# Mixture of experts after a chunked recurrence: one tile per step with its own weights, against two tiles per expert in a fixed order

## The chip, the cores and the metric

The kernel runs on one core of a Trainium2 chip. The metric is the device time of one execution in microseconds (us), a median over runs. The core has TensorE (PE, with its weight loads shown apart as PEld), VectorE (DVE), ScalarE (ACT), GpSimd (POOL) and SyncE (SP), which only issues transfers. All numbers are float32.

## The reference, cut to what matters

Part one is a recurrence over 768 steps for 4 batches of 8 heads with 40 by 40 states. Part two is a mixture of 16 experts in 4 groups; each of the 3072 tokens goes to one expert.

```python
for t in range(S):                                    # 768 steps
    y[:, :, t] = einsum('bhd,bhde->bhe', rt, state)
    Sa = einsum('bhde,bhe->bhd', state, at)
    state = state * wt[:, :, None, :] - einsum('bhd,bhe->bhde', Sa, bt) + einsum('bhd,bhe->bhde', vt, kt)
x = y.transpose(0, 2, 1, 3).reshape(3072, 320)
g_idx = argmax(x @ w_group)                           # 4 groups, softmax weight g_w
e_idx = argmax(xg @ w_expert[g])                      # 4 experts in the group, softmax weight e_w
h = maximum(xg[mask_e] @ w1[g, e], 0)                 # 320 -> 1024
out[tok_idx] = (g_w * e_w)[:, None] * (h @ w2[g, e])  # 1024 -> 320
```

With the reference's inputs the 16 experts get between 152 and 229 tokens each (204, 162, 213, 198, 203, 229, 197, 178, 211, 189, 202, 213, 152, 180, 174, 167), worked out from the reference.

## The kernel before, in words

**Part one** (lines 142 to 363) takes the recurrence in 24 chunks of 128 steps (6 chunks for each of 4 batches, the batches in turn). Each chunk loads six transposed inputs (`in_w`, `in_a`, `in_k`, `in_b`, `in_v`, `in_r`, three sets of buffers) and `vn` (two buffers) on SP's queue, forms triangular products, inverts by seven squarings (lines 267 to 299), and leaves 128 rows of the token matrix in `x_all`, which stays in SBUF. `gate_logits` transposes these rows and multiplies them with the gate weights. A check (lines 351 to 363) leaves two loop counts for a step-by-step version of the recurrence (lines 369 to 432); with these inputs both are zero.

**Routing** (lines 434 to 530) turns the gate logits of all tokens into a one-hot of 16 experts, counts with two matmuls against `up` and `ones`, gives every expert whole tiles of 128 rows in a DRAM buffer `xs`, and writes each token's row there, with its gate weight and number, by 24 indirect transfers on POOL's queue (line 528). `xs` was filled with blank rows at the start (line 189).

**The experts** (lines 532 to 572) are a loop over all NT = 39 tiles that could be needed. Each tile reads its expert's number from `ex_i`, loads that expert's 2,560 KB of weights (three buffers), loads its 128 rows (`xt`), transposes them, multiplies with `w1` (24 products of 128 columns, two matmul records each, 8 of the 24 on only 64 rows, since 320 = 128 + 128 + 64), applies relu, multiplies with `w2` (8 products of 320 columns, two records each), scales by the gate weight and writes the rows to `out` with an indirect transfer on POOL's queue.

The framework's scheduler sets the order of instructions on each engine and queue: an engine's queue runs in order, but that order is not the order of the program text. Tiles with `bufs=n` rotate over n buffers, and a load waits until the last reader of its buffer is done.

Of the kernel before, what the change touches and what calls it, by code (L numbers as in the profile page):

```python
# [25 lines left out]
def kernel(  # L26
# [28 lines left out]
    FG = 4  # L55
# [4 lines left out]
    XW = DM + 2  # L60
    NT = (NTOK + NE * (P - 1)) // P
# [21 lines left out]
    # up[s, t] = 1 for s < t; low[t, s] = 1 for s < t  # L83
# [13 lines left out]
    nc.gpsimd.iota(x_all[:, :, DM + 1:], pattern=[[P, NN], [1, 1]], base=0, channel_multiplier=1,  # L97
                   allow_small_or_imprecise_dtypes=True)
# [6 lines left out]
    # Rows sorted by expert, each expert's share filled up to whole tiles. Rows that no token  # L105
    # takes keep a zero vector and a number beyond the last token.
    xs = dpool.tile([NT * P, XW], F32, name="xs")
    blank = cpool.tile([P, XW], F32, name="blank")
    nc.vector.memset(blank, 0.0)
    nc.vector.memset(blank[:, DM + 1:], float(2 * NTOK))  # L110
# [16 lines left out]
    def gate_logits(pool, n):  # L127
        t = transpose_x(pool, x_all[:, n, :])
# [7 lines left out]
    # With P_t the product of w over the chunk's steps before t and Q_t that product through t,  # L136
    # A = a P, K = k / Q, B = b / Q and S the state at the chunk's start:
    #   (I + T) U = A S' + G V,         T[t, s] = B_s . A_t,  G[t, s] = K_s . A_t   (s < t)
    #   Y = P (R S + M K - N B),        M[t, s] = r_t . v_s,  N[t, s] = r_t . u_s   (s < t)
    #   next S = (S + V' K - U' B) Q_last  # L140
    # and (I + T)^-1 = (I - T)(I + T^2)(I + T^4)... exactly, T being strictly triangular.
    with ExitStack() as part:
# [18 lines left out]
        # The states of a pair of heads stand as the two diagonal blocks of a square that is zero  # L161
        # elsewhere: ST with the second axis of a state on the partitions, SN with the first.
# [14 lines left out]
        for u in range(NN):  # L177
# [4 lines left out]
            if u < NB:  # L182
                # the partitions that no head's rows take
# [14 lines left out]
            # the running products of w (within its bounds), and a, k, b scaled by them  # L198
# [57 lines left out]
            # the right-hand side, then a factor of the inverse at a time  # L256
# [52 lines left out]
            # the next state  # L309
# [13 lines left out]
            # what the chunk returns  # L323
            NTm = [product(UT, Rt, g, up4, "NT", 4) for g in GR]
            ps = small([P, H, D])
            for i in range(NP):
# [3 lines left out]
                for j in range(2):  # L330
# [19 lines left out]
            gate_logits(sb, n)  # L350

        # how often the bounds are broken
# [16 lines left out]
    with ExitStack() as part:  # L369
        sq = part.enter_context(tc.tile_pool(name="seq", bufs=1))  # L370
        x_seq = dpool.tile([NTOK, DM], F32, name="x_seq")
# [3 lines left out]
        # partition (q, b, h) holds rows q DQ .. (q + 1) DQ of the state of (b, h)  # L375
# [13 lines left out]
        with tc.For_i(0, n_seq, 1) as i:  # L389
# [34 lines left out]
            for b_ in range(B):  # L424
                r0 = nc.s_assert_within(s0 + b_ * S, 0, NTOK - TB)
                nc.sync.dma_start(out=x_seq[ds(r0, TB), :].rearrange("t (h d) -> h t d", h=H),
                                  in_=ys[b_ * H:(b_ + 1) * H])

        with tc.For_i(0, n_back, 1):
            nc.sync.dma_start(out=x_all[:, :, :DM], in_=x_seq.rearrange("(n p) d -> p n d", p=P))  # L430
            for n in range(NN):
                gate_logits(sq, n)

# [1 line left out]
    with ExitStack() as part:  # L435
# [6 lines left out]
        nc.gpsimd.iota(thr, pattern=[[P, NN]], base=0, channel_multiplier=0,  # L442
# [3 lines left out]
                       allow_small_or_imprecise_dtypes=True)  # L446
# [31 lines left out]
        nc.vector.tensor_tensor(x_all[:, :, DM], wtg, wte, op=ALU.mult)  # L478
        oh = gp.tile([P, NN, NE], F32, name="oh")
        for g in range(G):  # L480
# [3 lines left out]
        # each token's rank within its expert, then its row in xs  # L484
# [14 lines left out]
        cmp = gp.tile([P, NE, NN], F32, name="cmp")  # L499
        nc.vector.tensor_tensor(cmp, inc[:, :, NN - 1:].broadcast_to([P, NE, NN]),  # L500
                                thr[:, None, :].broadcast_to([P, NE, NN]), op=ALU.is_gt)
# [4 lines left out]
        base = gp.tile([P, NE, 1], F32, name="base")  # L506
        nc.vector.tensor_tensor(base[:, :, 0], tend, tiles, op=ALU.subtract)
        nc.vector.tensor_scalar(base, base, float(P), None, op0=ALU.mult)
        nc.vector.tensor_tensor(tot, tot, base.broadcast_to([P, NE, NN]), op=ALU.add)
        slot = gp.tile([P, NN, NE], F32, name="slot")  # L510
        nc.vector.tensor_tensor(slot, pr, tot.rearrange("p e n -> p n e"), op=ALU.add)
        nc.vector.tensor_tensor(slot, slot, oh, op=ALU.mult)
        pos = gp.tile([P, NN], F32, name="pos")
        nc.vector.tensor_reduce(out=pos, in_=slot, axis=AX.X, op=ALU.add)
        pos_i = cpool.tile([P, NN], I32, name="pos_i")
        nc.vector.tensor_copy(out=pos_i, in_=pos)

        # each tile's expert
        past = gp.tile([P, NT, NE], F32, name="past")
        nc.vector.tensor_tensor(past, tidx[:, :, None].broadcast_to([P, NT, NE]),  # L520
# [79 lines left out]
```

## Time and profile before

| what | value |
|---|---|
| median of 3 runs | 2348.99 us (2346.05 to 2349.27) |
| span of the profiled execution | 2344.1 us |
| TensorE busy | 2137.4 us (91%) |
| VectorE, ScalarE, GpSimd busy | 636.2, 416.2, 188.8 us |
| bytes moved | 152.68 MB, 65 GB/s over the span |
| mean granted TensorE clock | 0.806 of full |

The span runs from the first to the last instruction; the times of the runs are those of whole executions, 2.0 to 5.2 us longer than this span. The profiled execution's own whole time is not listed apart. The granted clock is 1.00 for 2.4 GHz and 0.50 for 1.2 GHz; a value between is a stretch with both.

### The profile page before, as it was taken

To read this page: it belongs to the slowest core of one execution; us is meant where nothing else is said; L and a number is where in the kernel's file an instruction comes from. 1 tells how busy PE (TensorE), PEld (TensorE's weight loads), DVE (VectorE), ACT (ScalarE), POOL (GpSimd) and SP (SyncE) were. 2 spreads that over 40 slices of the span, in tenths; PEclk is the share of its full clock that TensorE was granted. 3 is DMA by queue.
4 is the path that set the end of the run, shared out by engine and by line. 5 is a ranking of instruction groups with operands and counts; after the bars stand their busy time and mean duration, and the time that the engine had idled before them with its cause. 6 is when DMAs were issued, how large, how long until landed. Compare 5 with 4: busy or idle time off the path is not lost. (4 is left out here: it accounts for less than half of the span.)

```text
span 2344.1 us, 32451 instructions
## 1 busy us (share of the span) xinstructions
PE 2137.4 (91%) x13731; PEld 1943.0 (83%) x13731; DVE 636.2 (27%) x1156; ACT 416.2 (18%) x766; POOL 188.8 (8%) x190
## 2 busy tenths in 40 slices
PE   4999999999999999999999999999505999999998
PEld 3999999999999999999999999999404677777676
DVE  6423333332333333233333232222300111111111
ACT  2222222121222212122212122222000000000000
POOL 3000000000000000000000000000021000000000
PEclk9878876687877868787767787777656999999999
DMA  6000000000000000000000000000042666666661
GB/s 186 21 12 18 21 17 19 20 18 12 18 18 18 21 21 18 12 18 18 18 21 18 12 13 18 4 1 1 29 155 88 212 212 215 200 202 217 205 212 51
DMA packets 143699, 152.68 MB, mean 65 GB/s; under 512 B 33529, under 2 KB 129534, under 8 KB 143552
## 3 DMA queue, kind: packets, MB, share of 16 engines
q1 hardware_dynamic: 133824, 136.21, 18.9%
q10 hardware_dynamic: 6704, 6.46, 1.0%
q0 software_dynamic: 3024, 7.90, 0.9%
q8 instruction: 111, 1.82, 0.3%
q14 instruction: 36, 0.29, 0.0%
HBM read 136.22 MB, written 16.78 MB: 65 GB/s over the span
## 5 line engine op out<-in xcount | busy, mean ns | idle before, releaser
L558 PE MATMUL big<-xT,w1s 128*128 128x128 f32 x1872 | 338.9, 312 | 25.3 <-DVE xT L122 24.6
L558 PEld LDWEIGHTS big<-xT,w1s 128*128 128x128 f32 x1872 | 259.3, 191 | 108.0 <-DVE xT L122 34.7
L293 PE MATMUL small<-U,ET 128*128 128x40 f32 x2688 | 345.9, 290 | 0.6 <-ACT ET L276 0.4
L293 PEld LDWEIGHTS small<-U,ET 128*128 128x128 f32 x2688 | 340.8, 205 | 2.3 <-ACT ET L276 0.5
L273 PE MATMUL big<-ET,E 128*128 128x128 f32 x2304 | 336.6, 292 | 0.0
L273 PEld LDWEIGHTS big<-ET,E 128*128 128x128 f32 x2304 | 300.7, 204 | 0.0
L282 PE MATMUL big<-E,ET 128*128 128x128 f32 x1920 | 266.0, 284 | 0.0
L276 ACT COPY ET<-big 128x512 f32<-128x512 f32 x288 | 168.8, 586 | 481.2 <-PE big L273 481.2
L282 PEld LDWEIGHTS big<-E,ET 128*128 128x128 f32 x1920 | 247.3, 201 | 0.0
L299 DVE TENSOR_TENSOR U<-U,small 128x320 f32<-128x320 f32 x168 | 80.7, 480 | 457.4 <-PE small L293 457.4
L566 PE MATMUL small<-w2s,hT 128*128 128x320 f32 x624 | 180.5, 443 | 0.0
L566 PEld LDWEIGHTS small<-w2s,hT 128*128 128x128 f32 x624 | 116.6, 192 | 48.9 <-issue 1.6
L244 POOL TENSOR_TENSOR E<-E,fit 128x512 f32<-128x512 f32 x48 | 48.9, 1039 | 1199.5 <-DVE fit L242 1188.8
L561 DVE TENSOR_SCALAR hT<-big 128x512 f32<-128x512 f32 x39 | 27.0, 692 | 342.6 <-PE big L558 342.6
L124 ACT COPY xT<-big 64x128 f32<-64x128 f32 x63 | 16.3, 259 | 565.2 <-DVE xT L122 565.2
L120 PE MATMUL big<-ident,xt 128*128 128x128 f32 (+1 forms) x117 | 19.6, 277 | 96.4 <-DMA xt<-xs 96.4
L225 PE MATMUL big<-in_a,in_k 40*128 40x128 f32 x384 | 89.0, 447 | 18.1 <-DMA in_r<-in_rT_dram 18.1
L120 PEld LDWEIGHTS big<-ident,xt 128*128 128x128 f32 (+1 forms) x117 | 14.2, 133 | 105.4 <-DMA xt<-xs 97.5
L334 PE MATMUL small<-nB,NT 128*128 128x40 f32 x384 | 98.6, 351 | 0.0
L225 PEld LDWEIGHTS big<-in_a,in_k 40*128 40x128 f32 x384 | 75.1, 322 | 27.8 <-POOL in_k L212 18.1
L332 PE MATMUL small<-Kn,MT 128*128 128x40 f32 x384 | 94.4, 339 | 0.0
L263 PE MATMUL small<-vn,GT 128*128 128x40 f32 x384 | 94.1, 402 | 0.0
(166 smaller groups left out, 2302.5 us busy)
## 6 DMA issues: line engine op xcount, KB each, us to landing
w2s<-in_w_dram SPq DMA_DIRECT2D x39, 1280.0 KB
w1s<-in_w_dram SPq DMA_DIRECT2D x39, 1024.0 KB
w1s<-in_w_dram SPq DMA_DIRECT2D x39, 256.0 KB
xs<-blank ACTq DMA_DIRECT2D x1, 6279.0 KB
xt<-xs SPq DMA_DIRECT2D x39, 161.0 KB
vn<-in_v_dram SPq DMA_DIRECT2D x24, 160.0 KB
in_w<-in_wT_dram SPq DMA_DIRECT2D x48, 80.0 KB
in_a<-in_aT_dram SPq DMA_DIRECT2D x48, 80.0 KB
```

The lines of the kernel that those rows point to most:

```text
L225: nc.tensor.matmul(ps[:, q, :], lhsT=lhs[blk(g), q, :], rhs=rhs[blk(g), q, :], start=True, stop=True)
L244: nc.gpsimd.tensor_tensor(E[g], E[g], fit.broadcast_to([P, NP, P]), op=ALU.mult)
L263: nc.tensor.matmul(ps[:, 2 * i + j, :], lhsT=GT[j][:, i, :], rhs=vn[:, 2 * i + j, :], start=(c == 0), stop=(c == 0 or j == 1))
L273: nc.tensor.matmul(ps[:, q, :], lhsT=E[g][:, q, :], rhs=ET[g][:, q, :], start=True, stop=True)
L276: nc.scalar.copy(out=t, in_=ps)
L282: nc.tensor.matmul(ps[:, q, :], lhsT=ET[g][:, q, :], rhs=E[g][:, q, :], start=True, stop=True)
L293: nc.tensor.matmul(ps[:, h, :], lhsT=ET[h % 2][:, h // 2, :], rhs=U[:, h, :], start=True, stop=True)
L299: nc.vector.tensor_tensor(nx, U, ps, op=ALU.add if lv else ALU.subtract)
L332: nc.tensor.matmul(o, lhsT=MT[j][:, i, :], rhs=Kn[:, i, blk(j)], start=(c == 0), stop=False)
L334: nc.tensor.matmul(o, lhsT=NTm[j][:, i, :], rhs=nB[:, i, blk(j)], start=False, stop=(c == 0 or j == 1))
L558: nc.tensor.matmul(ps[:, f, :], lhsT=w1s[:kn, ko, (f0 + f) * P:(f0 + f + 1) * P], rhs=xT[:kn, ko, :], start=(ko == 0), stop=(ko == NK - 1))
L566: nc.tensor.matmul(ps, lhsT=hT[:, f, :], rhs=w2s[:, f, :], start=(f == 0), stop=(f == FQ - 1))
```

## The change

Token rows go from each chunk to a DRAM buffer `x_nat` in token order. Routing no longer moves rows. It gives every expert two tiles (TE = 2), and further tiles (up to NOV = 22) to experts with more than 256 tokens. One-hot matmuls over the 24 blocks of tokens give, for each row of each of the 54 possible tiles, the token's number and gate weight. The experts run in the order 0 to 15, both tiles together, with weights loaded once; rows are gathered from `x_nat` by index. The third part of `w1` and of the transposed rows is filled up with zeros to 128 rows. The weights of experts 0 and 1 are loaded during part one. A loop whose count is read on the chip takes further tiles.

```diff
-    x_all = cpool.tile([P, NN, XW], F32, name="x_all")
+    x_nat = dpool.tile([NTOK, DM], F32, name="x_nat")
...
+    WE = 2
+    KR = KO[-1][1]
+    wbuf = []
+
+    def weight_buffers(pool):
+        i = len(wbuf)
+        w1s = pool.tile([P, NK, F], F32, name=f"w1s{i}", bufs=1)
+        w2s = pool.tile([P, FQ, DM], F32, name=f"w2s{i}", bufs=1)
+        nc.gpsimd.memset(w1s[KR:, NK - 1, :], 0.0)
+        wbuf.append((w1s, w2s))
+
+    for i in range(WE):
+        weight_buffers(cpool)
+
+    def load_weights(e, buf):
+        w1s, w2s = buf
+        nc.sync.dma_start(out=w1s[:, :NK - 1, :],
+                          in_=w1_flat[ds(e * DM, (NK - 1) * P), :].rearrange("(o p) f -> p o f", p=P))
+        nc.sync.dma_start(out=w1s[:KR, NK - 1, :], in_=w1_flat[ds(e * DM + (NK - 1) * P, KR), :])
+        nc.sync.dma_start(out=w2s, in_=w2_flat[ds(e * F, F), :].rearrange("(o p) d -> p o d", p=P))
...
-            if u == NB:
-                nc.scalar.dma_start(out=xs.rearrange("(j p) d -> p j d", p=P),
-                                    in_=blank[:, None, :].broadcast_to([P, NT, XW]))
+            if NB < u <= NB + WE:
+                load_weights(u - NB - 1, wbuf[u - NB - 1])
...
+            xn = sb.tile([P, DM], F32, name="xn")
...
-            gate_logits(sb, n)
-
-        # how often the bounds are broken
+            nc.sync.dma_start(out=x_nat[n * P:(n + 1) * P, :], in_=xn)
+            gate_logits(sb, xn, n)
...
+        slot = gp.tile([P, NN, NE], F32, name="slot")
+        nc.vector.tensor_tensor(slot, pr, tot.rearrange("p e n -> p n e"), op=ALU.add)
+        nc.vector.tensor_tensor(slot, slot, oh, op=ALU.mult)
+        rank = gp.tile([P, NN], F32, name="rank")
+        nc.vector.tensor_reduce(out=rank, in_=slot, axis=AX.X, op=ALU.add)
...
+        ov_t = gp.tile([P, NE], F32, name="ov_t")
+        nc.vector.tensor_tensor(ov_t, tend, tiles, op=ALU.subtract)
+        nc.vector.tensor_scalar(ov_t, ov_t, float(NM - TE), None, op0=ALU.add)
+        nc.vector.tensor_tensor(ov_t, ov_t, own_t, op=ALU.subtract)
+
+
+        ge = gp.tile([P, NN, NN], F32, name="ge")
+        nc.vector.tensor_tensor(ge, rank[:, :, None].broadcast_to([P, NN, NN]),
+                                thr[:, None, :].broadcast_to([P, NN, NN]), op=ALU.is_ge)
+        nth = gp.tile([P, NN], F32, name="nth")
+        nc.vector.tensor_reduce(out=nth, in_=ge, axis=AX.X, op=ALU.add)
...
+        nc.vector.tensor_tensor(slot, oh, ov_t[:, None, :].broadcast_to([P, NN, NE]), op=ALU.mult)
+        nc.vector.tensor_reduce(out=tl, in_=slot, axis=AX.X, op=ALU.add)
+        nc.vector.tensor_tensor(tl, tl, ge[:, :, TE - 1], op=ALU.mult)
+        nc.vector.tensor_tensor(slot, oh, own_t[:, None, :].broadcast_to([P, NN, NE]), op=ALU.mult)
+        nc.vector.tensor_reduce(out=rank, in_=slot, axis=AX.X, op=ALU.add)
+        nc.vector.tensor_tensor(tl, tl, rank, op=ALU.add)
+        nc.vector.tensor_tensor(tl, tl, nth, op=ALU.add)
+
+
+        oh_row = gp.tile([P, NN, P], F32, name="oh_row")
+        nc.vector.tensor_tensor(oh_row, row[:, :, None].broadcast_to([P, NN, P]),
+                                lane[:, None, :].broadcast_to([P, NN, P]), op=ALU.is_equal)
+        what = gp.tile([P, NN, 2, NT], F32, name="what")
+        nc.vector.tensor_tensor(what[:, :, 1, :], tl[:, :, None].broadcast_to([P, NN, NT]),
+                                tidx[:, None, :].broadcast_to([P, NN, NT]), op=ALU.is_equal)
+        nc.gpsimd.tensor_tensor(what[:, :, 0, :], what[:, :, 1, :],
+                                tok1[:, :, None].broadcast_to([P, NN, NT]), op=ALU.mult)
+        nc.vector.tensor_tensor(what[:, :, 1, :], what[:, :, 1, :],
+                                gw[:, :, None].broadcast_to([P, NN, NT]), op=ALU.mult)
+        ps = small([P, 2, NT])
+        for n in range(NN):
+            nc.tensor.matmul(ps.rearrange("p a j -> p (a j)"), lhsT=oh_row[:, n, :],
+                             rhs=what[:, n, :, :].rearrange("p a j -> p (a j)"),
+                             start=(n == 0), stop=(n == NN - 1))
...
-        for n in range(NN):
-            nc.gpsimd.indirect_dma_start(
-                out=xs[:, :], out_offset=bass.IndirectOffsetOnAxis(ap=pos_i[:, n:n + 1], axis=0),
-                in_=x_all[:, n, :], in_offset=None)
...
+        fp = part.enter_context(tc.tile_pool(name="ffn", bufs=2))
+        weight_buffers(fp)
+        WB = len(wbuf)
+        XB = []
+        for i in range(2):
+            t = fp.tile([P, NK, TE * P], F32, name=f"xT{i}", bufs=1)
+            nc.gpsimd.memset(t[KR:, NK - 1, :], 0.0)
+            XB.append(t)
+
+        def ffn(buf, xT, cols, weight, dst):
+
+            w1s, w2s = buf
+            n_t = len(cols)
+            w = n_t * P
+            per = 512 // w
+            for t_, col in enumerate(cols):
+                xt = fp.tile([P, DM], F32, name="xt", bufs=4)
+                nc.gpsimd.indirect_dma_start(
+                    out=xt, out_offset=None, in_=x_nat[:, :],
+                    in_offset=bass.IndirectOffsetOnAxis(ap=col, axis=0))
+                pt = big([P, NK, P])
+                for ko, (k0, kn) in enumerate(KO):
+                    nc.tensor.transpose(pt[:kn, ko, :], xt[:, k0:k0 + kn], ident)
+                sl = slice(t_ * P, (t_ + 1) * P)
+                nc.vector.tensor_copy(out=xT[:, :NK - 1, sl], in_=pt[:, :NK - 1, :])
+                nc.scalar.copy(out=xT[:KR, NK - 1, sl], in_=pt[:KR, NK - 1, :])
+            hT = fp.tile([P, FQ, TE * P], F32, name="hT")
+            for f0 in range(0, FQ, per):
+                ps = big([P, per, w])
+                for f in range(per):
+                    for ko in range(NK):
+                        nc.tensor.matmul(ps[:, f, :], lhsT=w1s[:, ko, (f0 + f) * P:(f0 + f + 1) * P],
+                                         rhs=xT[:, ko, :w], start=(ko == 0), stop=(ko == NK - 1))
...
+            for t_ in range(n_t):
+                ps = small([P, DM])
+                for f in range(FQ):
+                    nc.tensor.matmul(ps, lhsT=hT[:, f, t_ * P:(t_ + 1) * P], rhs=w2s[:, f, :],
+                                     start=(f == 0), stop=(f == FQ - 1))
+                yt = fp.tile([P, DM], F32, name="yt", bufs=3)
+                nc.vector.tensor_scalar(yt, ps, weight[t_], None, op0=ALU.mult)
+                nc.gpsimd.indirect_dma_start(
+                    out=out[:, :], out_offset=bass.IndirectOffsetOnAxis(ap=dst[t_], axis=0),
+                    in_=yt, in_offset=None, bounds_check=NTOK - 1, oob_is_err=False)
...
+        for e in range(NE):
+            if e >= WE:
+                load_weights(e, wbuf[e % WB])
+            js = range(e * TE, (e + 1) * TE)
+            ffn(wbuf[e % WB], XB[e % 2], [column(src_i, j) for j in js],
+                [column(w_row, j) for j in js], [column(dst_i, j) for j in js])
+
+
+        n_over = nc.values_load(n_ov[0:1, 0:1], min_val=0, max_val=NOV)
+        with tc.For_i(0, n_over, 1) as j:
```

## Rows read from the trace of the kernel before

**Rows 1.** The page's first line: span and instructions.
```profile
span 2344.1 us, 32451 instructions
```
**Rows 2.** Stretches: us, busy time (instructions) by engine, clock, DMA share, GB/s.
```profile
0.00:18.10 18.10, 0.00 (x0) 0.00 (x0) 15.25 (x28) 11.62 (x18) 11.21 (x30) 1.00 0.66 173
...
1670.00:1693.00 23.00, 3.03 (x5) 1.18 (x4) 14.88 (x51) 0.74 (x3) 0.38 (x3) 0.50 0.01 3
1693.00:1782.50 89.50, 0.91 (x4) 0.49 (x4) 0.86 (x4) 0.23 (x1) 23.19 (x24) 0.50 0.42 138
1782.50:1805.00 22.50, 21.94 (x67) 15.90 (x67) 1.54 (x3) 0.63 (x2) 0.02 (x1) 0.57 0.18 59
1805.00:2336.20 531.20, 507.16 (x2543) 373.69 (x2543) 61.13 (x149) 32.55 (x76) 37.36 (x38) 1.00 0.60 195
2336.20:2344.10 7.90, 0.00 (x0) 0.00 (x0) 0.55 (x1) 0.00 (x0) 0.98 (x1) 0.80 0.00 0
```
**Rows 3.** Timeline of one expert tile: start us, us, engine, line, instruction [idle before].
```profile
1805.08 8.52 PE L558 MATMUL big<-xT,w1s 128*128 128x128 f32 x48 [0.65 <-DVE xT L122]
...
1813.54 4.58 PE L566 MATMUL small<-w2s,hT 128*128 128x320 f32 x16
...
1817.95 0.49 PE L120 MATMUL big<-ident,xt 128*128 128x128 f32 x3
...
1819.09 8.52 PE L558 MATMUL big<-xT,w1s 128*128 128x128 f32 x48 [0.65 <-DVE xT L122]
```
**Rows 4.** Timeline of PE's weight loads at the first tile's start.
```profile
1782.46 0.93 PEld L558 LDWEIGHTS big<-xT,w1s 128*128 128x128 f32 x4 [1.14 <-issue]
1783.61 0.50 PEld L558 LDWEIGHTS big<-xT,w1s 64*128 64x128 f32 x2 [0.22 <-issue]
1784.34 0.93 PEld L558 LDWEIGHTS big<-xT,w1s 128*128 128x128 f32 x4 [0.23 <-issue]
```
**Rows 5.** Timeline of PE's weight loads in part one, at full clock.
```profile
1648.74 1.87 PEld L273 LDWEIGHTS big<-ET,E 128*128 128x128 f32 x16
```
**Rows 6.** Timeline of DVE in the routing.
```profile
1686.61 0.55 DVE L500 TENSOR_TENSOR cmp<-inc,thr 128x384 f32<-128x384 f32 x1
...
1688.10 0.80 DVE L520 TENSOR_TENSOR past<-tidx,tend 128x624 f32<-128x624 f32 x1
...
1690.24 1.09 DVE L511 TENSOR_TENSOR slot<-small,tot 128x384 f32<-128x384 f32 x1
```
**Rows 7.** The page's group of POOL multiplies: count, busy us, mean ns, idle before.
```profile
L244 POOL TENSOR_TENSOR E<-E,fit 128x512 f32<-128x512 f32 x48 | 48.9, 1039 | 1199.5 <-DVE fit L242 1188.8
```
**Rows 8.** Timeline of POOL: three of the 24 row scatters.
```profile
1693.02 1.15 POOL L528 DMA_INDIRECT xs<-x_all,pos_i  x1 [18.11 <-DVE pos_i L516]
1699.85 0.96 POOL L528 DMA_INDIRECT xs<-x_all,pos_i  x1 [5.68 <-DMA xs<-x_all,pos_i]
...
1723.07 0.96 POOL L528 DMA_INDIRECT xs<-x_all,pos_i  x1 [1.89 <-DMA xs<-x_all,pos_i]
```
**Rows 9.** Timeline around the two loops that run no iteration.
```profile
1670.58 0.65 DVE L381 TENSOR_TENSOR sel<-sel,ident 128x32 f32<-128x32 f32 x3
1674.54 0.14 POOL L439 IOTA rank_i<- 128x4 f32 x1 [63.23 <-DVEq L429]
```
**Rows 10.** Timeline of the start of the kernel.
```profile
0.83 1.11 SPq L196 DMA_DIRECT2D vn<-in_v_dram  x2
...
2.13 2.26 SPq L194 DMA_DIRECT2D in_w<-in_wT_dram  x2
...
13.29 0.38 ACTq L189 DMA_DIRECT2D xs<-blank  x1
...
43.31 1.12 PE L247 MATMUL big<-ident,E 128*128 128x128 f32 x4 [10.60 <-POOL E L244]
```
**Rows 11.** Timeline of SP's queue in part one.
```profile
221.82 0.39 SPq L196 DMA_DIRECT2D vn<-in_v_dram  x1
...
254.15 0.69 SPq L194 DMA_DIRECT2D in_w<-in_wT_dram  x2
```

More of the change, by code (lines that the diff above doesn't have):

```diff
@@ L425 @@
                 r0 = nc.s_assert_within(s0 + b_ * S, 0, NTOK - TB)
-                nc.sync.dma_start(out=x_seq[ds(r0, TB), :].rearrange("t (h d) -> h t d", h=H),
+                nc.sync.dma_start(out=x_nat[ds(r0, TB), :].rearrange("t (h d) -> h t d", h=H),
                                   in_=ys[b_ * H:(b_ + 1) * H])
         with tc.For_i(0, n_back, 1):
-            nc.sync.dma_start(out=x_all[:, :, :DM], in_=x_seq.rearrange("(n p) d -> p n d", p=P))
             for n in range(NN):
-                gate_logits(sq, n)
+                xn = sq.tile([P, DM], F32, name="xn", bufs=2)
+                nc.sync.dma_start(out=xn, in_=x_nat[n * P:(n + 1) * P, :])
+                gate_logits(sq, xn, n)
     with ExitStack() as part:
@@ L477 @@
         ohe, wte = choose(el, "e")
-        nc.vector.tensor_tensor(x_all[:, :, DM], wtg, wte, op=ALU.mult)
+        gw = gp.tile([P, NN], F32, name="gw")
+        nc.vector.tensor_tensor(gw, wtg, wte, op=ALU.mult)
         oh = gp.tile([P, NN, NE], F32, name="oh")
@@ L505 @@
         nc.vector.tensor_tensor_scan(tend, ones[:, :NE], tiles, 0.0, op0=ALU.mult, op1=ALU.add)
[L506 to L520, printed above, removed]
-                                tend[:, None, :].broadcast_to([P, NT, NE]), op=ALU.is_ge)
@@ new lines @@
+        nth = gp.tile([P, NN], F32, name="nth")
+        nc.vector.tensor_reduce(out=nth, in_=ge, axis=AX.X, op=ALU.add)
+        row = gp.tile([P, NN], F32, name="row")
+        nc.vector.tensor_scalar(row, nth, -float(P), None, op0=ALU.mult)
+        nc.vector.tensor_tensor(row, row, rank, op=ALU.add)
+        tl = gp.tile([P, NN], F32, name="tl")
+        nc.vector.tensor_tensor(slot, oh, ov_t[:, None, :].broadcast_to([P, NN, NE]), op=ALU.mult)
+        nc.vector.tensor_reduce(out=tl, in_=slot, axis=AX.X, op=ALU.add)
@@ new lines @@
+        ps = small([P, 2, NT])
[3 more added lines that the diff above has]
+                             start=(n == 0), stop=(n == NN - 1))
+        w_row = cpool.tile([P, NT], F32, name="w_row")
+        nc.scalar.copy(out=w_row, in_=ps[:, 1, :])
+        src_i = cpool.tile([P, NT], I32, name="src_i")
+        dst_i = cpool.tile([P, NT], I32, name="dst_i")
@@ new lines @@
+        nc.vector.tensor_scalar(src_i, ps[:, 0, :], -1.0, 0.0, op0=ALU.add, op1=ALU.max)
+        none = gp.tile([P, NT], F32, name="none")
+        nc.vector.tensor_scalar(none, ps[:, 0, :], 0.5, float(2 * NTOK), op0=ALU.is_lt, op1=ALU.mult)
+        tokf = gp.tile([P, NT], F32, name="tokf")
+        nc.vector.tensor_scalar(tokf, ps[:, 0, :], -1.0, None, op0=ALU.add)
+        nc.vector.tensor_tensor(dst_i, tokf, none, op=ALU.add)
+        past = gp.tile([P, NOV, NE], F32, name="past")
+        nc.vector.tensor_tensor(past, tidx[:, :NOV, None].broadcast_to([P, NOV, NE]),
+                                tend[:, None, :].broadcast_to([P, NOV, NE]), op=ALU.is_ge)
@@ L533 @@
+        nc.vector.tensor_copy(out=n_ov, in_=tend[:, NE - 1:])
     with ExitStack() as part:
-        wp = part.enter_context(tc.tile_pool(name="weights", bufs=3))
-        fp = part.enter_context(tc.tile_pool(name="ffn", bufs=3))
-        for j in range(NT):
-            er = nc.sync.value_load(ex_i[0:1, j:j + 1], min_val=0, max_val=NE - 1)
+        fp = part.enter_context(tc.tile_pool(name="ffn", bufs=2))
[6 more added lines that the diff above has]
+            XB.append(t)
@@ new lines, in ffn @@
+        def ffn(buf, xT, cols, weight, dst):
[21 more added lines that the diff above has]
+                                         rhs=xT[:, ko, :w], start=(ko == 0), stop=(ko == NK - 1))
+                if (f0 // per) % 2:
+                    nc.vector.tensor_relu(hT[:, f0:f0 + per, :w], ps)
+                else:
+                    nc.scalar.activation(hT[:, f0:f0 + per, :w], ps, ACT.Relu)
+            for t_ in range(n_t):
[8 more added lines that the diff above has]
+                    in_=yt, in_offset=None, bounds_check=NTOK - 1, oob_is_err=False)
@@ new lines, in column @@
+        def column(t, j):
+            return t[:, j:j + 1]
+        for e in range(NE):
[6 more added lines that the diff above has]
+        with tc.For_i(0, n_over, 1) as j:
+            j = nc.s_assert_within(j, 0, NOV - 1)
+            er_i = fp.tile([P, 1], I32, name="er_i", bufs=1)
+            nc.vector.tensor_copy(out=er_i, in_=ex_i[:, ds(j, 1)])
+            er = nc.sync.value_load(er_i[0:1, 0:1], min_val=0, max_val=NE - 1)
@@ L538 @@
             r1 = nc.s_assert_within(er * DM, 0, (NE - 1) * DM)
             r2 = nc.s_assert_within(er * F, 0, (NE - 1) * F)
[L540 removed]
+            w1s, w2s = wbuf[0]
             src = w1_flat[ds(r1, DM), :]
```

78 lines of the change are left out of this document (31 added, 47 removed).

## The prediction

> **What bounds the kernel now.** I read the page first (a span of 2344.1 us [rows 1]), then cut the span into stretches [rows 2]. Up to 1670 us the recurrence runs. From 1670.0 to 1693.0 the routing runs on DVE (14.88 of 23 us busy) with PE almost idle. From 1693.0 to 1782.5 nothing computes: rows are scattered to `xs`. From 1782.5 to 2336.2 (553.7 us) the 39 expert tiles run, PE busy, and a tail of 7.9 us follows. So the change has three targets: the idle 89.5 us, the 553.7 us, and whatever it adds to the 23 us.
>
> Inside the experts PE sets the pace. One tile takes 14.0 us in the timeline [rows 3]: `w1` from 1805.08 to 1813.54 (8.46), `w2` to 1817.95 (4.41), then three transposes and a wait of 0.65 for their copies (1.14 to 1819.09). The transfers keep up, at 195 GB/s and a share of 0.60 of the engines [rows 2].
>
> **The experts.** Each expert gets at most 229 tokens, so two tiles hold them: 32 tiles instead of 39, and the new loop has no iteration.
>
> `w2` stays 16 records per tile, 4.41 us each, 8.8 us for two; that is 0.276 us per record of 320 columns.
>
> `w1` goes from 48 records per tile to 48 per pair of tiles, with 256 columns instead of 128 and always 128 rows. The trace has no 256-column record, so I bound it. A record of 128 columns takes 8.46/48 = 0.176 us here, but 1.87/16 = 0.117 us in part one at the same full clock [rows 5]. What differs shows at the first tile, which ran at half clock [rows 2, 4]: four 128-row weight loads in 0.93 us, then 0.22 idle, two 64-row loads in 0.50, then 0.23 idle. The idle stands only where rows change from 128 to 64 and back, and twice in six records it explains the slow average. With all loads on 128 rows it goes. Then the rate is by columns: 0.276 x 256/320 = 0.221 us; a line through 0.117 (128 columns) and 0.276 (320) gives 0.223. I take 0.221: 48 x 0.221 = 10.6 us. If the difference 0.176 - 0.117 = 0.059 were a fixed cost of accumulating into one place, it would be 0.280, 13.4 us. That is a rival below.
>
> The timeline shows the switch, the Trainium skill explains it: "TensorEngine Tiling (Array Packing)", Key Properties, says that a change of tiling mode drains TensorE. By that rule `w1` is 10.6 us and the sum stands; without it the fixed-cost rival has a hold.
>
> Transposes: 1.14 for the first tile and about 0.49 for three more, 1.6 us. An expert is then 10.6 + 8.8 + 1.6 = 21.0 us, and 16 of them 336 us. Relu and scaling double in columns per expert, not per tile, and stay below 2 us per 21 us on DVE and ACT (61.13 and 32.55 us in 531.2 now [rows 2]). Weights: 2.56 MB per 21 us is 122 GB/s, against 195 now, so they are hidden. The first tile took 22.5 us instead of 14.0 because PE had idled and the clock was at half, 0.57 on average, until `w2`'s denser records came [rows 2]. In the new kernel PE again idles just before. If `w1`'s 256 columns bring the clock up soon, about 2 us are lost, if its whole stage runs at half, 10.6. I take 4. Experts: 340 instead of 553.7, a gain of **213.7**.
>
> **The routing.** The 24 scatters and the read of `xs` go (89.5 us). What comes instead is longer on DVE. Prices: 0.55 us for 384 elements, 0.80 for 624, 1.09 where the operand is in PSUM [rows 6], so 1.04 ns per element beyond 0.15; POOL takes 1039 ns for 512 [rows 7]. From the end of `tot` (about 1686.7) the chain is: `slot` 1.09 + 0.56, `rank` 0.55; `cmp`, `tiles`, `tend` and three small ones for `ov_t` 1.8; `ge` and `nth` (576 elements) 1.5; `row` 0.4; `tl` 2.8 (four of 384, three small); `oh_row` (3072) 3.35; `what` (1296) 1.5 on DVE, 2.6 on POOL, 1.5 on DVE again. Sum 17.7, to 1704.4. Then 24 matmuls, 48 records of 108 columns: at half clock a load is 0.93/4 = 0.233 us [rows 4], so 11.2 us, to 1715.6; at full clock it would be 5.6. Small copies and the pools' hand-over: 1717.
>
> The gather is new: an indirect transfer that reads. The nearest row is the scatter [rows 8]: 0.96 to 1.15 to issue, then 1.89 to 5.68 until the next may go (long while weights are loading, short after). I take 4, bounds 1.9 and 5.7. Both gathers have landed at 1722 to 1723, transposes at half clock and copies take 2.5: `w1` of expert 0 starts at 1725 instead of 1782.5, a gain of **57.5**, 50 to 66 by the bounds (full clock in the matmuls and a quick gather above, both slow and some DVE operations slower on broadcasts below). The Trainium skill prices such a transfer at about 2.0 us plus bytes/436e3 ("DMA: Bandwidth & Descriptors", Anatomy of one DMA), an estimate of 2.4 us for 164 KB, by which the sum would be 2 us lower; the row decides, as it holds contention with weights.
>
> Later gathers and writes: 64 on POOL in 340 us, 1 us each to issue, so POOL has room. With four `xt` buffers an expert's two gathers can go a whole expert (21 us) ahead; they cost nothing then. If that cover is gone, PE waits.
>
> **Part one.** `xn` to `x_nat`: 24 stores of 160 KB on SP's queue. They wait for a chunk's end, and the queue runs in order, so loads behind them wait too. Vectors for a chunk are loaded long ahead: a chunk's loads run from 221.82 to 254.15 [rows 11], spread over the work that frees their buffers, with three sets in turn. I cost the stores at nothing. The start: before, the 6.3 MB of blank rows issued at 13.29 delayed the third chunk's inputs, behind which DVE and then PE stood for 10.60 us [rows 10]; this goes. But 5.1 MB of weights take their place on SP's queue. SP took `vn` of the second chunk before the first chunk's `in_w` [rows 10], so what is ready goes first, and the weights are ready at once. At the 195 GB/s of the expert stage [rows 2] they hold the first inputs up 26 us if they go first, of which the 11 above come back. Behind the inputs, they cost nothing. So -11 to +15; I take 0.
>
> **The tail.** 7.9 us remain, and the loop that doesn't run comes before. Two such loops took from 1671.2 to 1674.5 [rows 9], 3.3 us; for one, with its count read from memory and a wait for the last writes, I take 3, bounds 1 to 8.
>
> **The sum.** 2344.1 - 57.5 - 213.7 + 3 = 2075.9 us of span. The median of the runs shown is 4.9 above the span: **2080**.
>
> **The rivals.** (a) A fixed cost per `w1` record: 48 x 0.059 x 16 = 45 us more, 2125. For it speaks that 0.176 was measured in this very loop; against it that the idle stands only at the changes of rows. (b) The gathers come late: if POOL's queue has an expert's gathers behind the previous expert's scaled write, PE waits about 1 + 1 + 4 us per expert, 15 x 6 = 90, 2170. The Trainium skill adds for such gaps, in "TensorE: Matmul & The Clock Gate", Why this matters for your kernels, that idle stretches between matmul bursts bring the lower clock back. As a mechanism of this kernel: idle before the first tile went with half clock through its whole `w1` stage [rows 2, 4]; at 10.6 us of loss per expert on top, 15 x 16.6 = 249, 2330, still just faster. (c) Slower than before: `x_nat`'s store stands ahead of the next chunk's loads on SP's queue. Then each chunk starts with loading: the first one needed from 2.13 to 18.1 us before PE began [rows 2, 10], 16 us, and 22 or 23 such waits are 360: 2440. It decides against the change from about 12 us per chunk. Against it: SP's queue showed order by readiness, not by text [rows 10], and three sets of inputs. (d) The change doesn't do what it says: an expert over 256 tokens would bring loop iterations, each about 13 us of loading and 14 of work unhidden; with 229 at most it can't be.
>
> **How the numbers follow.** My forecast, with the start's and the gather's bounds, 0.76: 2050 to 2105. Rival (a) 0.08, (b) without the clock 0.06, with it 0.02, (c) 0.05. The remaining 0.03 is for something slow in the expert stage that no row shows. Low end: 11 from the start, 8 from the routing, and 15 x 1 if some transposes move under `w2`: 2045. High end: rival (a) with 10 more from the start, 2135. That leaves some 2 in 10 out. Changes within 0.2% (about what a measurement of this kernel can tell) would take an accident: 0.01. Slower 0.06, faster 0.93.
>
> **What would show it.** In the new profile: 256-column records at 0.22 us apart and no idle between weight loads within `w1` (right), 0.28 (rival a); experts 21 us apart; the first `w1` near 1725, and before it 48 records at half clock; PE idle before each expert's transposes waiting on `xt` (rival b); PE idle at each chunk's start on `in_` tiles (rival c); weights before or behind `in_w` on SP's queue in the first 20 us. The prediction is wrong if part one's length changes by more than 15 us or the experts' 340 us are off by more than 30.

## The result and the profile after

The kernel after takes 2060.26 us (median, 2058.56 to 2067.16) against 2349.13 us for the kernel before on the same chip: ratio 0.878, 95% interval 0.8764 to 0.8796. That is faster, inside the forecast range, and 20 us below the forecast of 2080.

The page of the kernel after, its span and the busy time of PE:

```profile
span 2057.5 us, 29577 instructions
...
PE 1942.0 (94%) x12542; PEld 1820.6 (88%) x12542; DVE 635.0 (31%) x1113; ACT 411.5 (20%) x755; POOL 194.7 (9%) x196
```

The span fell from 2344.1 [rows 1] to 2057.5, by 286.6 us. The same cut into stretches as [rows 2], in the kernel after: the routing on DVE, the 48 records of the one-hot matmuls, the gathers, the first expert, the other fifteen, the tail.

```profile
1663.70:1697.80 34.10, 3.44 (x6) 1.57 (x6) 23.58 (x67) 0.74 (x3) 3.11 (x7) 0.50 0.01 2
1697.80:1706.20 8.40, 8.35 (x48) 8.18 (x48) 0.00 (x0) 0.00 (x0) 0.00 (x0) 0.65 0.00 0
1706.20:1717.80 11.60, 1.78 (x6) 0.90 (x6) 1.52 (x6) 0.46 (x2) 6.58 (x9) 0.68 0.81 282
1717.80:1738.30 20.50, 20.45 (x80) 16.27 (x81) 1.93 (x3) 1.45 (x3) 1.76 (x2) 0.93 0.27 89
1738.30:2046.70 308.40, 298.62 (x1291) 236.95 (x1289) 47.22 (x90) 25.66 (x60) 55.72 (x56) 1.00 0.39 133
2046.70:2057.50 10.80, 0.00 (x0) 0.00 (x0) 0.55 (x1) 0.00 (x0) 0.98 (x1) 0.74 0.02 6
```

The reader sees that the idle stretch of 89.5 us is gone, that 20 us of matmuls and gathers stand in its place, that PE is busy through the experts at a granted clock of 1.00, and that the DMA share there fell to 0.39. One expert, two tiles, in PE's timeline of the kernel after:

```profile
2006.91 10.63 PE L633 MATMUL big<-xT,w1s 128*128 128x256 f32 x48 [0.65 <-DVE xT L626]
...
2017.37 8.78 PE L642 MATMUL small<-w2s,hT 128*128 128x320 f32 x32
...
2025.99 0.82 PE L624 MATMUL big<-ident,xt 128*128 128x128 f32 x6
...
2027.45 10.23 PEld L633 LDWEIGHTS big<-xT,w1s 128*128 128x128 f32 x48 [0.92 <-DVE xT L626]
```

From 2006.91 to 2027.46 is 20.55 us, against 2 x 14.0 for two tiles before [rows 3]. The weight loads of `w1` now stand in one piece of 48 with no idle inside, where [rows 4] had idle at every change between 128 and 64 rows.

### The profile page after: what moved, and what is told of

It is laid out like the page before. It is cut to its first block, busy times and chain, and to the rows that moved or that the text cites. A ratio compares the mean times of both kernels' runs of the same rounds, so it can differ in the third digit from the quotient of the medians.

```text
span 2057.5 us, 29577 instructions
## 1 busy us (share of the span) xinstructions
PE 1942.0 (94%) x12542; PEld 1820.6 (88%) x12542; DVE 635.0 (31%) x1113; ACT 411.5 (20%) x755; POOL 194.7 (9%) x196
## 3 DMA queue, kind: packets, MB, share of 16 engines
q1 hardware_dynamic: 99648, 73.42, 11.9%
## 5 line engine op out<-in xcount | busy, mean ns | idle before, releaser
L633 PE MATMUL big<-xT,w1s 128*128 128x256 f32 x768 | 171.4, 383 | 10.3 <-DVE xT L626 10.3
L633 PEld LDWEIGHTS big<-xT,w1s 128*128 128x128 f32 x768 | 145.6, 191 | 34.2 <-DVE xT L626 14.8
L642 PE MATMUL small<-w2s,hT 128*128 128x320 f32 x512 | 140.4, 432 | 0.0
L642 PEld LDWEIGHTS small<-w2s,hT 128*128 128x128 f32 x512 | 97.3, 190 | 38.8
L302 DVE COPY E<-big 128x512 f32<-128x512 f32 x96 | 66.2, 691 | 100.1 <-PE big L296 98.5
L300 ACT COPY E<-big 128x512 f32<-128x512 f32 x144 | 84.3, 585 | 50.4 <-PE big L296 50.4
L277 PEld LDWEIGHTS small<-vn,GT 128*128 128x128 f32 x384 | 91.8, 333 | 0.9 <-DVE E L242 0.7
L348 PEld LDWEIGHTS small<-nB,NT 128*128 128x128 f32 x384 | 87.7, 281 | 2.3 <-DVE NT L242 2.3
```

The lines of the kernel that those rows point to most:

```text
L277: nc.tensor.matmul(ps[:, 2 * i + j, :], lhsT=GT[j][:, i, :], rhs=vn[:, 2 * i + j, :], start=(c == 0), stop=(c == 0 or j == 1))
L300: nc.scalar.copy(out=t, in_=ps)
L348: nc.tensor.matmul(o, lhsT=NTm[j][:, i, :], rhs=nB[:, i, blk(j)], start=False, stop=(c == 0 or j == 1))
L633: nc.tensor.matmul(ps[:, f, :], lhsT=w1s[:, ko, (f0 + f) * P:(f0 + f + 1) * P], rhs=xT[:, ko, :w], start=(ko == 0), stop=(ko == NK - 1))
L642: nc.tensor.matmul(ps, lhsT=hT[:, f, t_ * P:(t_ + 1) * P], rhs=w2s[:, f, :], start=(f == 0), stop=(f == FQ - 1))
```

## The experiments

Each is shown by its edit, what was expected, what was measured and what follows. The time between the start of one expert's (or tile's) `w1` and the next, read from PE's timeline, is called the step.

**1. The padding alone, in the kernel before.**

```diff
-            w1s = wp.tile([P, NK, F], F32, name="w1s")
+            w1s = W1[j % 3]      # three fixed buffers, rows 64 to 127 of the third part zero
...
-                        nc.tensor.matmul(ps[:, f, :], lhsT=w1s[:kn, ko, (f0 + f) * P:(f0 + f + 1) * P],
-                                         rhs=xT[:kn, ko, :], start=(ko == 0), stop=(ko == NK - 1))
+                        nc.tensor.matmul(ps[:, f, :], lhsT=w1s[:, ko, (f0 + f) * P:(f0 + f + 1) * P],
+                                         rhs=xT[:, ko, :], start=(ko == 0), stop=(ko == NK - 1))
```

> The kernel before with one part of the change alone: the third part of w1 and of the transposed rows is filled up with zeros to 128 rows, so every w1 record is on 128 rows; 39 tiles, scatters and loads stay. If the switch between 128 and 64 rows costs 0.176 - 0.117 us per record, w1 falls from 8.46 to 5.6 us a tile, a tile from 14.0 to 11.15 us, and the time by 39 x 2.85 = 111 us to about 2238. If the 0.176 us is a fixed cost of accumulating into one place, the time stays at 2349. If transfers become the bound (2.72 MB in 11.15 us are 244 GB/s), something between, with PE waiting for w1s or xt.

Measured: 2230.29 us, ratio 0.951 (0.9468 to 0.9553). PE's timeline of this kernel, one tile:

```profile
2006.67 5.62 PE L568 MATMUL big<-xTp,w1p 128*128 128x128 f32 x48 [0.65 <-DVE xTp L561]
2012.13 4.47 PE L576 MATMUL small<-w2s,hT 128*128 128x320 f32 x16
2016.44 0.49 PE L559 MATMUL big<-ident,xt 128*128 128x128 f32 x3
2017.58 5.62 PE L568 MATMUL big<-xTp,w1p 128*128 128x128 f32 x48 [0.65 <-DVE xTp L561]
```

The step is 10.91 us instead of 14.0; `w1` takes 5.46 instead of 8.46, 0.114 us per record of 128 columns. The fixed cost of accumulating is refuted: same places, same columns, and the 0.059 us per record are gone. At this pace transfers did not become the bound of every step; 25 of 37 steps are 10.9, but 11 are 11.1 to 11.9, with PE slower or pausing inside `w2`. What it waits for there is not shown.

**2. The padding undone, in the kernel after.**

```diff
-                    for ko in range(NK):
-                        nc.tensor.matmul(ps[:, f, :], lhsT=w1s[:, ko, (f0 + f) * P:(f0 + f + 1) * P],
-                                         rhs=xT[:, ko, :w], start=(ko == 0), stop=(ko == NK - 1))
+                    for ko, (_, kn) in enumerate(KO):
+                        nc.tensor.matmul(ps[:, f, :], lhsT=w1s[:kn, ko, (f0 + f) * P:(f0 + f + 1) * P],
+                                         rhs=xT[:kn, ko, :w], start=(ko == 0), stop=(ko == NK - 1))
```

> The kernel after with the padding undone: the third part of w1 is on 64 rows again, the rest stays. If the switch drains at 256 columns as it did at 128, 16 switches per expert cost 0.177 us each, 2.8 us per expert, 45 us in all, 2105. If the longer stream of 256 columns hides the switch, or if it was a fixed cost of accumulating, the time stays at 2060.

Measured: 2127.92 us, ratio 0.9064 (0.9028 to 0.9101), 68 us above the kernel after. The weight loads of this kernel in PE's timeline:

```profile
2020.66 0.29 PEld L633 LDWEIGHTS big<-xT,w1s 64*128 64x128 f32 x2 [0.33 <-issue]
2021.28 0.73 PEld L633 LDWEIGHTS big<-xT,w1s 128*128 128x128 f32 x4 [0.33 <-issue]
2022.34 0.29 PEld L633 LDWEIGHTS big<-xT,w1s 64*128 64x128 f32 x2 [0.33 <-issue]
```

Idle stands again before each change, 0.33 us at full clock, and six records take 1.68 us (2020.66 to 2022.34) instead of 6 x 0.2135 = 1.28. The step is 23.68 instead of 20.55, 50 us over sixteen. The longer stream does not hide the switch, and it does not make it dearer: 3.13 us for the 16 changes of an expert are 0.20 us each, and experiment 1 took away 3.09 us for the 16 changes of a tile, 0.19 each. The 0.177 in the expectation was too low, because it was worked out from 0.117 us per record where 0.114 was measured, and left out that `w2` behind the last change also takes 0.1 us longer. The Trainium skill, in "TensorEngine Tiling (Array Packing)", Key Properties, says that a change of tiling mode drains TensorE; these rows, with idle at every change between 128 and 64 rows, agree. About 14 us more come from the first expert, whose step is 37.97. The stretches of that expert (busy time of PE, PEld, DVE, ACT, POOL, then clock, DMA share, GB/s):

```profile
1722.00:1726.00 4.00, 4.00 (x9) 2.07 (x8) 0.00 (x0) 0.00 (x0) 0.23 (x1) 0.50 0.23 69
...
1746.00:1750.00 4.00, 4.00 (x9) 2.46 (x8) 0.69 (x1) 0.00 (x0) 0.00 (x0) 0.50 0.92 312
1750.00:1754.00 4.00, 4.00 (x13) 2.70 (x13) 0.47 (x1) 0.00 (x0) 0.00 (x0) 0.80 0.07 15
```

PE counts as busy all the time and stayed at 1.2 GHz until after 1750, when `w2` ran. In the first tile of the kernel before, too, the clock rose only in `w2`, at about 1802. In the kernel after, without switches, the clock was full from about 1721:

```profile
1718.00:1720.00 2.00, 2.00 (x5) 1.64 (x6) 0.00 (x0) 0.08 (x1) 0.54 (x1) 0.50 0.48 144
1720.00:1722.00 2.00, 2.00 (x9) 1.67 (x9) 0.00 (x0) 0.00 (x0) 0.00 (x0) 0.82 0.04 8
1722.00:1724.00 2.00, 2.00 (x11) 1.77 (x10) 0.00 (x0) 0.60 (x1) 0.00 (x0) 1.00 0.00 0
```

**3. Two tiles of one expert, but `w1` with 128 columns.**

```diff
-                    for ko in range(NK):
-                        nc.tensor.matmul(ps[:, f, :], lhsT=w1s[:, ko, (f0 + f) * P:(f0 + f + 1) * P],
-                                         rhs=xT[:, ko, :w], start=(ko == 0), stop=(ko == NK - 1))
+                    for t_ in range(n_t):
+                        sl = slice(t_ * P, (t_ + 1) * P)
+                        for ko in range(NK):
+                            nc.tensor.matmul(ps[:, f, sl], lhsT=w1s[:, ko, (f0 + f) * P:(f0 + f + 1) * P],
+                                             rhs=xT[:, ko, sl], start=(ko == 0), stop=(ko == NK - 1))
```

> The kernel after with w1 tile by tile: 96 records of 128 columns per expert instead of 48 of 256, all on 128 rows. If a 128-column record is bound by its weight load, 0.117 us, w1 takes 11.2 us instead of 10.25 and the time is 16 us longer, 2076. With a fixed cost per record it is 96 x 0.176 = 16.9 us, 106 us longer, 2166.

Measured: 2065.02 us, ratio 0.8799 (0.8762 to 0.8835), no difference from the kernel after that these intervals can tell. PE's timeline:

```profile
2008.87 10.98 PE L635 MATMUL big<-xT,w1s 128*128 128x128 f32 x96 [0.32 <-DVE xT L626]
2019.69 8.78 PE L644 MATMUL small<-w2s,hT 128*128 128x320 f32 x32
2028.30 0.82 PE L624 MATMUL big<-ident,xt 128*128 128x128 f32 x6
2029.44 10.98 PE L635 MATMUL big<-xT,w1s 128*128 128x128 f32 x96 [0.32 <-DVE xT L626]
```

The step is 20.57 against 20.55. The `w1` stage is 10.82 us (0.113 per record) against 10.46 between the stage starts of the kernel after, and 0.33 of that comes back, because `w1` can begin on the first tile's rows while the second's are still copied (a wait of 0.32 instead of 0.65). My 16 us was too high: the record took 0.113, not 0.117, and I had not counted the shorter wait. So the 256-column records, the most visible part of the change, bring nothing here; with all loads on 128 rows, a record of 128 columns takes little more than half of one of 256 (0.113 against 0.218 between the stage starts).

**4. The gathers' cover taken away.**

```diff
-                xt = fp.tile([P, DM], F32, name="xt", bufs=4)
+                xt = fp.tile([P, DM], F32, name="xt", bufs=1)
```

> The kernel after with one xt buffer instead of four, so a gather can't start before the transposes of the tile before it: the cover of the gathers is gone for the second tile of each expert. An issue of 1 us and 3 to 5 us to land are then a wait of PE of 4 to 6 us per expert: 16 x 5 = 80, about 2140, with w1 at full clock. If such a wait brings the clock down for the following w1 stage, up to 10 us more per expert, up to 2300.

Measured: 2196.68 us, ratio 0.9354 (0.9317 to 0.9392), 136 us above the kernel after, between the two cases. Timeline rows, then stretches of this kernel:

```profile
2013.88 0.98 POOL L619 DMA_INDIRECT xt<-x_nat,src_i  x1 [3.03 <-PE big L624]
...
2015.16 1.01 POOL L646 DMA_INDIRECT out_dram<-yt,dst_i  x1 [0.30 <-issue]
...
2019.83 0.87 PE L624 MATMUL big<-ident,xt 128*128 128x128 f32 x3 [6.22 <-DMA xt<-x_nat,src_i]
```

```profile
2013.00:2021.00 8.00, 1.48 (x8) 0.67 (x5) 1.14 (x3) 0.26 (x1) 2.01 (x3) 0.77 0.58 194
2021.00:2033.00 12.00, 11.78 (x48) 10.18 (x49) 0.86 (x2) 1.45 (x3) 0.95 (x1) 0.87 0.05 15
...
1750.00:2184.00 434.00, 338.14 (x1291) 261.55 (x1289) 48.63 (x90) 25.68 (x60) 58.71 (x59) 0.85 0.29 96
```

From the second expert on PE waits 3.8 to 6.5 us before the second tile's transposes, 88 us together (101 with the first expert's gathers); steps are 26.3 to 30.2. The rest is the clock: it fell during each wait, and `w1`'s first part ran at 1.2 GHz (0.85 over the experts instead of 1.00). This is the wait of rival (b), brought about by fewer buffers: both of its prices are real, but the clock's is 2 to 3 us per expert instead of 10.6, because in this `w1` without switches the full clock was back after some 4 us (0.96 in 2140 to 2142, in a stage begun at 2135.95). The Trainium skill, in "TensorE: Matmul & The Clock Gate", Why this matters for your kernels, says that idle gaps between matmul bursts bring the lower clock back; these rows agree. The last two waits are 3.76 and 3.79 us and all others but those 5.9 or more: after the last weight load, issued at 2101.83, no weights share the engines with the gathers. In the kernel after, four buffers keep it off: PE waits for `xt` only before the first expert.

**5. The last loop left out** (with it the tiles beyond an expert's second, of which these inputs have none): `values_load` and the `For_i` at the end are removed.

> The kernel after without its last loop and the load of its count (it leaves out tiles beyond the second of an expert, of which there are none here). The tail between the last w2 record and the span's end was forecast to be 3 us longer by the loop: 2057. If the loop costs nothing the time stays at 2060, and the tail at 10.8 us.

Measured: 2063.07 us, ratio 0.8791 (0.8763 to 0.882), nothing by the median. But the tail, from the last `w2` record to the end of the span, is 8.0 us instead of 10.8:

```profile
2000.00:2048.50 48.50, 47.20 (x200) 36.55 (x198) 6.84 (x13) 3.42 (x8) 4.96 (x5) 1.00 0.03 13
2048.50:2056.50 8.00, 0.02 (x1) 0.00 (x0) 0.55 (x1) 0.00 (x0) 0.98 (x1) 0.83 0.02 6
```

So this loop without an iteration costs 2.8 us; the total can't show it, for a reason that experiment 9 gives.

**6. The write of blank rows put back** in part one, where nothing reads it.

```diff
+            if u == NB:
+                nc.scalar.dma_start(out=xs.rearrange("(j p) d -> p j d", p=P),
+                                    in_=blank[:, None, :].broadcast_to([P, 39, DM + 2]))
```

> The kernel after with the 6.3 MB write of blank rows put back at its old place, where nothing reads them. If the 5.9 us by which part one ended earlier came from that write's absence, the time goes up by about 6 us to 2066 and PE waits some 10 us again near 43 us. If they came from elsewhere it stays at 2060.

Measured: 2068.29 us, ratio 0.8816 (0.8785 to 0.8847). PE waits 9.00 us again at the same place:

```profile
31.67 1.12 PE L268 MATMUL big<-ident,E 128*128 128x128 f32 x4 [4.87 <-POOL E L265]
41.79 1.11 PE L268 MATMUL big<-ident,E 128*128 128x128 f32 x4 [9.00 <-POOL E L265]
```

Yet part one ended at 1664.2 us against 1664.1 in the kernel after (the first instruction behind the loop counts, DVE's `st`). The rows of the second chunk (`xn`) were already level. First the kernel after, with the stretch from 43 to 100 us, then this kernel:

```profile
157.05 0.49 DVE L351 TENSOR_TENSOR xn<-small,Pn 128x320 f32<-128x320 f32 x1 [6.50 <-PE small L348]
...
43.00:100.00 57.00, 55.35 (x391) 53.58 (x390) 25.23 (x41) 12.14 (x22) 2.51 (x2) 0.78 0.36 106
```

```profile
156.49 0.49 DVE L358 TENSOR_TENSOR xn<-small,Pn 128x320 f32<-128x320 f32 x1 [3.24 <-PE small L355]
...
43.00:100.00 57.00, 55.01 (x430) 52.69 (x430) 29.55 (x46) 14.75 (x27) 5.90 (x4) 0.93 0.45 129
```

With the wait the granted clock was 0.93 in that stretch, without it 0.78: PE fell to 1.2 GHz between 90 and 100 us instead of between 70 and 80, and did the missing work at the higher clock meanwhile. So in this execution the clock gave a visible wait of 9 us back within two chunks. The medians can't tell whether it always does.

**7. Weights not loaded ahead.** First with `WE = 0` alone (the two buffers kept).

> The kernel after with no weights loaded during part one (WE = 0, buffers in the same places). The first load then starts where the third did, about 1707 us, and 2.56 MB at 200 GB/s take 13 us: the first w1 starts at about 1722 instead of 1717.9, 4 us later if the gathers share the engines well, 10 if they slow each other down: 2064 to 2070. If the loads of weights at the start had cost part one something, part one ends earlier than 1663.7 us.

Measured: 2069.91 us, ratio 0.8806 (0.8772 to 0.884). This leaves the question open: SP's queue still loaded both experts at the start, since the buffers were free.

```profile
54.01 0.39 SPq L122 DMA_DIRECT2D w1s<-in_w_dram  x1
54.44 0.56 SPq L124 DMA_DIRECT2D w1s<-in_w_dram  x1
55.05 0.58 SPq L125 DMA_DIRECT2D w2s<-in_w_dram  x1
```

Then with a dependence on the routing's result:

```diff
+        for w1s, w2s in wbuf:
+            nc.vector.tensor_copy(out=w1s[:, 0, 0:1], in_=tend[:, 0:1])
+            nc.vector.tensor_copy(out=w2s[:, 0, 0:1], in_=tend[:, 0:1])
```

> The kernel after with the weights of experts 0 and 1 held back until the routing: their buffers get a first element from the routing's result, so that no load can run ahead (with WE = 0 alone they were still loaded at 54 to 58 us). Three experts' weights, 7.7 MB, then start at about 1687 us and the first 2.56 MB need 13 us: there by 1700, before the gathers. Then only the gathers suffer, behind 5 MB more until about 1720: 0 to 10 us, 2060 to 2070. If the gather's 6 us in the kernel after are its own, nothing changes.

Measured: 2063.34 us, ratio 0.8787 (0.8763 to 0.8812). From part one's end to the first `w1` it took 53.3 us, against 53.7 in both profiles of the kernel after (experiment 9 has the second). Loading the first experts' weights during part one brought nothing here: their loads were issued from 1690.32 to 1695.75 us, and 5 MB fit into the routing.

**8. Rows transposed ahead, and the first gathers with fewer loads beside them.** `rows_ahead` splits the gather and transposes off `ffn` into `rows` and calls it for the next expert between `w1` and `w2`; zero fills go to the start or behind the first gathers; the one-hot gets a tile of its own.

```diff
+            def following():
+                rows(XB[(e + 1) % 2], [column(src_i, j + TE) for j in js])
...
+            if then:
+                then()
             for t_ in range(n_t):
                 ps = small([P, DM])
...
-        nc.gpsimd.tensor_tensor(what[:, :, 0, :], what[:, :, 1, :],
+        nc.gpsimd.tensor_tensor(what[:, :, 0, :], eq,
```

> The kernel after with three things more: the next expert's rows are transposed between w1 and w2 of this one, the zero fills of POOL stand ahead of part one or behind the first gathers, and the products with the token's number (POOL) and with the gate weight (DVE) start from a tile of their own and run side by side. 0.65 us of PE's wait per expert goes, 10 us; 1.5 us for the fills, 1.5 for the products: 13 us less, 2047. If the wait for the copies is only moved (behind w1's last relu), 2057.

Measured: 2048.3 us, ratio 0.8726 (0.8696 to 0.8757). The step fell to 19.63, by 0.92, more than the 0.65 of the wait. The routing won nothing (53.8 us to the first `w1`). Three rows of this kernel say why:

```profile
1697.01 3.61 POOL L575 TENSOR_TENSOR what<-eq,tok 128x1296 f32<-128x1296 f32 x1 [23.66 <-DVE eq L573]
...
1711.11 1.15 POOL L614 DMA_INDIRECT xt<-x_nat,src_i  x1 [10.49 <-DVE dst_i L593]
...
1718.15 0.87 PE L619 MATMUL big<-ident,xt 128*128 128x128 f32 x3 [9.01 <-DMA xt<-x_nat,src_i]
```

POOL's product took 3.61 us instead of 2.36 in the kernel after, where DVE did not work beside it (it also reads a tile of its own now; the two were not tested apart). And the gather took 7.0 us from issue to the first transpose, although it was issued 1.5 us sooner after its indices: it shared the engines with the third expert's weights. `gather_first` holds most of these back:

```diff
+                weight_buffers(fp)
+                for t in wbuf[-1]:
+                    nc.vector.tensor_copy(out=t[:, 0, 0:1], in_=xt[:, 0:1])
```

> rows_ahead with the third expert's weights held back until the first expert's second gather has landed. If the 7.0 us from the first gather's issue to the first transpose come from sharing the engines with those 2.56 MB, they fall to 3 to 4 us and the time to about 2045; if they are the gather's own latency, both stay (2048).

Measured: 2049.74 us, ratio 0.8714 (0.8691 to 0.8738). Its rows:

```profile
1716.53 0.50 SPq L129 DMA_DIRECT2D w1s<-in_w_dram  x1
...
1717.42 1.15 POOL L614 DMA_INDIRECT xt<-x_nat,src_i  x1 [10.04 <-DVE dst_i L593]
...
1720.63 0.87 PE L619 MATMUL big<-ident,xt 128*128 128x128 f32 x3 [5.17 <-DMA xt<-x_nat,src_i]
```

Now 3.2 us from issue to transpose: of the 7.0, 3.8 were contention. The gather was not quite alone: the third part of `w1`, 256 KB, was not held back and went 0.9 us ahead of it. From part one's end to the first `w1` it took 49.7 us. The median does not show these 4 us over `rows_ahead`; 1.6 of them went again in the first step, 22.75 us against 21.16. Both kernels beat the kernel before, and the kernel after by under 1%.

**9. The kernel after once more.**

> The kernel after once more, on the same chip as gather_first and in five rounds: 2060, some 12 us above rows_ahead's 2048. It also shows how far part one's end (1663.7 us in the first profile) moves from one execution to the next with no change at all; if it stays within 1 us, part one's 5.9 us came from the change.

Measured: 2067.98 us, ratio 0.8784 (0.876 to 0.8808). The first instruction behind part one's loop counts, in the first profile of the kernel after and, in the second fence, in this one:

```profile
1664.13 0.39 DVE L392 MEMSET st<- 128x400 f32 x1 [0.20 <-DVE loops L379]
```

```profile
1675.75 0.39 DVE L392 MEMSET st<- 128x400 f32 x1 [0.20 <-DVE loops L379]
```

The same program's part one took 11.6 us longer. Chunk by chunk its rows came between 2.9 us earlier and 5.1 us later up to the fifteenth chunk, 1.9 us later there, and lost the rest in the last nine; from 1200 to 1663 us the granted clock was 0.74 against 0.75. So part one's 6.0 us between before and after are not shown to come from the change. The two medians of this one program, 2060.26 and 2067.98, are 7.7 us apart, so effects below some 8 us must be read from the stage where they arise, not from the total.

## Why the prediction was right, point by point

**The sum in spans.** The 286.6 us divide so: experts 224.8 (553.7 to 328.9), routing from part one's end to the first `w1` 58.7 (112.4 to 53.7), tail -2.9, part one 6.0. Forecast: 213.7, 57.5, -3, 0. The rest of the 20 us is the time outside the span, 2.8 us now for 4.9 assumed. Part one's 6.0 are within what one program moves by itself, and the second measurement of the kernel after lies only 12 us below the forecast.

**The experts** were the term that was mis-sized, by 11 us. A step was forecast at 21.0 and is 20.55: `w1` 10.46 for 10.6, `w2` 8.62 for 8.8, transposes and wait 1.47 for 1.6. That is 7.2 us over sixteen. The allowance of 4 us for the half clock was too large, by 2.6: the first step is 21.94, 1.4 more than the others, as the clock was full about 3 us into `w1` (in the second profile of this kernel about 5.7 us, and the step 23.33). The last 1.3 us are one expert's transposes, which I had counted both in the routing and in the experts.

**Where the 224.8 come from** could only be told by the experiments: seven tiles fewer at 14.0 are 98.0; padding, 3.09 per tile by experiment 1, is 98.9 for 32 tiles; two tiles in one go (two steps of 10.91 against one of 20.55) 20.3; the first step 7.2. My step "what differs is the switch of rows" was right and shown from both sides (experiments 1 and 2), with 0.19 to 0.20 us per change for my 0.177. My step from 128 to 256 columns was right in size and without effect (experiment 3). The 20.3 are 1.27 us per pair: 0.81 from transposes and wait (1.47 against twice 1.14) and 0.46 from `w1` (10.46 against twice 5.46); `w2` gives nothing (8.62 against twice 4.31). With 128 columns and both tiles together the step is the same, so the gain is that of going through the stages once per pair, not of the longer record.

**The routing** came out 1.2 us from the forecast, partly by luck, with errors that cancel: the 48 records took 8.35 us instead of 11.2, because the clock rose during them (0.65 on average); POOL's zero fills of `w1s` and `xT`, not in my sum, delayed the first gather by 1.5 us; and the gather was 1.2 us longer than assumed. The DVE prices held: `oh_row` 3.36 for 3.35, `what` 1.51 for 1.5, POOL's product 2.36 for 2.6. The gather took 6.2 us from issue to transpose for 5 assumed; with most of the weights held back 3.2 (experiment 8). The estimate of 2.4 us from "DMA: Bandwidth & Descriptors", Anatomy of one DMA, in the Trainium skill is 0.8 us below the row with little beside it and 3.8 below the contended one.

**Part one.** The stores cost nothing that shows: SP waited 223.7 us on `xn` in total, up to 69.2 at a time, and from 50 us on PE never waited over 0.6 us at a time, so rival (c) did not come about. Weights went behind the first inputs (issued from 39.98 us). The wait of 10.60 us at the start went, as forecast, but the term "-11" took the wait for its price: experiment 6 brings it back, and the higher clock behind it makes it up within two chunks. In the kernel before, with the same wait and a clock of 0.96 from 43 to 100 us, the second chunk's rows came at 163.32 us, 6.3 later than in the kernel after, and part one ended 6.0 later. As one program moves by 11.6, whether the write of blank rows ever cost something stays open.

**The tail** was right: 2.8 for 3 (experiment 5). Rival (a) is refuted by experiment 1, rival (d) by the trace: the loop ran no iteration.

## What to carry to other kernels

If matmuls of different row counts alternate in a loop, look for idle between weight loads at each change; filling up to 128 rows with zeros saved 3 us in a step of 14 here. A wait that goes is not always time gained: look at the granted clock behind it. Before joining tiles to get longer records, check whether the short record already covers its weight load: here 128 columns nearly did, and the joining of records was worth nothing, while fewer tiles and fewer waits gained time. A gather takes longer when it shares the engines with a bulk load (7.0 us against 3.2 here): a load that is not urgent can be held back until the first gather has landed. That gained 4 us of the routing, which the total did not show.

## What the runs showed of the hardware that was not expected

- A busy PE can stay at 1.2 GHz: with a change of rows twice in six records, `w1`'s first stage ran at 0.50 for 28 us, PE counted as busy without a gap; without these changes the clock was full about 3 us into the same stage, in a second execution about 5.7 us.
- The same program's part one, 1.66 ms of PE work with hardly a wait, ended 11.6 us apart in two executions. A wait of 9 us put into its start was made up by 157 us, at a granted clock of 0.93 instead of 0.78 in between.
- POOL's product of 1296 elements took 3.61 us with DVE working beside it, and 2.36 alone and from another tile.
- A gather of 128 rows took 7.0 us from issue to first use beside a load of weights, and 3.2 with most of that load held back.
